# Token pairs for k and q of batch 0 and k of batch 1, one maximum and one exponential per part in batch 0, and another order of the head of a fused attention and MLP kernel

## The chip, the cores and the metric

One core of a Trainium2 chip runs the whole kernel. The metric is the device time of one execution in microseconds. Times of several executions are given as a median with the lowest and the highest. One further execution was taken by the hardware profiler; its time and its trace are used for the working, and they are a little longer than the median run. On this kernel a change of less than 0.2% cannot be told from none.

## The reference, cut to what matters

```python
# q, k, v: (8 batches, 8 heads, 576 tokens, 64);  p: (8, 8, 32, 64), float32
def sm_attn(qq, kk, vv):
    s = (1 / 8) * qq @ kk.T
    a = exp(s - max(s, axis=-1))
    a = a / (sum(a, axis=-1) + 1e-9)
    return a @ vv
p_packed = sm_attn(p, k, v)              # 32 packed rows per head
out = sm_attn(q, p_packed, p_packed)     # back to 576 tokens
x = out as (4608 tokens, 512)
h = x @ w_in                             # w_in (512, 1024), float64 in memory
solu = h * softmax(h)
ln = (solu - mean) / sqrt(var + 1e-6) * g_ln
return ln @ w_out                        # w_out (1024, 512), float64 in memory
```

## The kernel before, in words

**Steps and their order.** Every piece of work is a named step. `add` registers it with what it needs (`after`) and with the buffers that it takes and gives back; `perform` then emits the steps in the order of the long string `ORDER`, and `issue` ties each engine's instructions to that order. So an engine never overtakes itself: when a step waits, all that stands behind it on the same engine waits too. The loads, the transposing DMAs and the stores are all issued by SyncE (SP) in that order, into one queue. A name is step, then batch or `w` after a slash, or a token tile after a dash: `kt0/1` is for batch 1, `wa3/w` belongs to the weights, `m1-5` is for token tile 5.

**Weights (`/w`).** `w_in` and `w_out` come as 64-bit floats, in four pieces of 1 MB each: `lw0` to `lw3` for `w_in`, `lW0` to `lW3` for `w_out` (L215). For each piece, `wa` and `wl` take the high and the low word apart on ScalarE (ACT; L230, L234), `wm` joins the magnitude on VectorE (DVE; L239), `wp` sums columns on TensorE (PE; L249), and `ws` puts the sign in on DVE (L256). Two maxima follow: `wb` for `w_in` (L259) and `pw` for `w_out` (L316 to L322). For each of the eight slices of `w_out`, `ch`, `cm` and `cl` then make the fp16 high and low parts `wch` and `wcl` (L330, L340 to L343, L334).

**Attention of a batch (`/0` to `/7`).** The loads are `lk`, `lq` and `lv`. In batch 0, k and q are loaded as rows of token pairs for tokens 0 to 511 (L127, 512 bytes in a run) and two loads for the last 64 tokens (L135), turned by PE in the steps `ka` and `qa` (L151, L153) and copied by ACT in `kc` and `qc` (L159, L161). In all other batches k and q come in four parts each with runs of 128 bytes (L412), and DVE turns them in 32 by 32 blocks, four steps `kt` and four `qt` each (L428). `s10` and `s11` are the scores of the packed rows for even and odd heads (L441 for batch 0, L451 else), `mx` their row maxima (L456 for each half of 288 columns, L458 to join them), `ex` the exponentials (L469 for each half, with sums), `es` and `rs` the sums and their reciprocals. `tp`, `tc` and `av` turn the exponentials and multiply by v (L488, L495, L505). `pp` scales (L514), `pt` and `pc` turn the packed rows (L524, L528), `pe`, `pk`, `to` and `un` find a power-of-two unit (L519 to L359). `sx` are the second scores (L547, L554), `sb`, `sm`, `su`, `se`, `ss`, `sn` the second softmax (L559 to L579), `at`, `ah`, `al` give the weights as fp16 high and low parts `a2h` and `a2l` (L618 to L633). `z0` and `z1` multiply the packed rows by `w_in` (L590), `zh` and `zl` store the product as fp16 high and low parts (L606 on ACT, L614 on DVE).

**Token tile (36 of 128 tokens).** `m1` is h: 12 products of 128 by 512 into one of two h buffers (L721). `nm` is the row maximum (L725, L727), `bd` a bound (L733 to L736), `ex` the exponential on ACT (L741), `u` the product on DVE (L746), `mu` the mean on GpSimd (POOL; L750), `yh` and `yl` the fp16 high and low parts (L754, L757), `tr` a transposing DMA (L761), `sq` and `cr` the row factor (L765 to L773). `m2a` and `m2b` are the second product, 24 of 128 by 512, all into one PSUM buffer (`NPO = 1`, L780); `ev` scales and copies it out (L784), `st` stores it. The first four tiles (0 to 3) belong to batch 0; tile 4 is half of batch 0 and half of batch 1.

The shape of the head is thus: weights and batch 0's attention must come before the first `m1`; the parts of `w_out` must be ready before the first `m2a`.

Of the kernel before, what the change touches and what calls it, by code (L numbers as in the profile page):

```python
# [34 lines left out]
tp0/0 tc0/0 tp1/0 tc1/0 tp2/0 qa1/0 qa2/0 qc1/0 lW2/w wp4/w qa3/0 ws4/w lv/0 tc2/0 av/0 wa6/w wl6/w qc2/0 es1/0
rs/0 lW3/w qc3/0 wp5/w ws5/w lP/w wm6/w lk0/1 pp/0 pe/0 lk1/1 pt/0 pc/0 wp6/w ws6/w sx0/0 sb0/0 sm0/0 sx1/0
wa7/w sb1/0 pk/0 wl7/w wm7/w su0/0 z0/0 to/0 se0/0 un/0 z1/0 wp7/w zh0/0 pw/w ko/w lq0/1 sm1/0 su1/0 ch5/w
lk2/1 lq1/1 lq2/1 ch4/w cm4/w cm5/w se1/0 ss0/0 sn0/0 lk3/1 at0/0 pa/w ss1/0 ch2/w pd/w px/w cm2/w kt0/1 zl0/0
ch3/w ch0/w zh1/0 ah0/0 kt1/1 ch1/w kt2/1 sn1/0 cl2/w cm0/w at1/0 cl4/w cm3/w cl0/w ah1/0 cl3/w kt3/1 s10/1
zl1/0 al0/0 al1/0 cl5/w cm1/w m1-0 mx0/1 ex0/1 ws7/w es0/1 ch6/w s11/1 m1-3 lq3/1 cl1/w cm6/w qt0/1 nm-0 lv0/1  # L40
mx1/1 lk0/2 lv1/1 lv2/1 lk1/2 bd-0 qt1/1 qt2/1 qt3/1 ex-0 u-0 ex1/1 tp0/1 es1/1 rs/1 tp1/1 tc0/1 tc1/1 mu-0
tp2/1 tc2/1 av/1 nm-3 pp/1 ch7/w cm7/w pt/1 yh-0 yl-0 tr-0 bd-3 pc/1 m1-2 ex-3 sq-0 lk2/2 lk3/2 u-3 cl6/w mu-3
pe/1 cl7/w nm-2 gd/w lv0/2 sx0/1 sb0/1 sm0/1 m1-1 yh-3 yl-3 ex-2 pk/1 to/1 tr-3 su0/1 se0/1 bd-2 un/1 z0/1
zh0/1 sq-3 lq0/2 ss0/1 u-2 zl0/1 kt0/2 m2a-0 m2b-0 mu-2 yh-2 lq1/2 yl-2 sx1/1 cr-0 ev-0 sb1/1 sm1/1 sn0/1 st-0
kt1/2 su1/1 m2a-3 sq-2 cr-3 kt2/2 tr-2 z1/1 kt3/2 se1/1 ss1/1 zh1/1 m2b-3 zl1/1 at0/1 ev-3 sn1/1 ah0/1 al0/1
at1/1 ah1/1 s10/2 mx0/2 ex0/2 lq2/2 lq3/2 nm-1 ex-1 bd-1 m2a-2 al1/1 s11/2 mx1/2 ex1/2 m1-5 u-1 tp0/2 tp1/2
lv1/2 tc0/2 cr-2 qt0/2 lk0/3 tc1/2 tp2/2 nm-5 lk1/3 qt1/2 tc2/2 ex-5 m2b-2 bd-5 es0/2 mu-1 yh-1 st-3 es1/2
lv2/2 u-5 mu-5 rs/2 qt2/2 yh-5 av/2 pp/2 pe/2 yl-5 sq-5 qt3/2 m1-6 tr-5 pt/2 pc/2 pk/2 sx0/2 yl-1 nm-6 m1-4
sq-1 ev-2 sb0/2 bd-6 sm0/2 su0/2 to/2 sx1/2 sb1/2 sm1/2 un/2 su1/2 ex-6 u-6 mu-6 lv0/3 m2a-5 z0/2 zh0/2 nm-4
bd-4 m2b-5 tr-1 m1-7 lv1/3 cr-5 zl0/2 z1/2 se0/2 ev-5 ss0/2 sn0/2 yh-6 yl-6 sq-6 cr-1 lk2/3 lk3/3 kt0/3 kt1/3  # L50
st-2 m2a-1 se1/2 m2b-1 zh1/2 ex-4 lk0/4 kt2/3 tr-6 kt3/3 ss1/2 lq0/3 sn1/2 lq1/3 zl1/2 s10/3 at0/2 cr-6 ev-1
at1/2 ah0/2 al0/2 ah1/2 mx0/3 lv2/3 nm-7 st-1 ex0/3 es0/3 u-4 mu-4 ex-7 m2a-6 s11/3 mx1/3 m2b-6 ex1/3 bd-7
tp0/3 tp1/3 tp2/3 yh-4 ev-6 u-7 es1/3 lk1/4 st-5 yl-4 al1/2 tc0/3 tc1/3 tc2/3 lq2/3 lq3/3 m1-9 qt0/3 qt1/3 nm-9
# [816 lines left out]
```

## Time and profile before

| | |
|---|---|
| median of 3 runs | 417.19 us (416.96 to 417.67) |
| profiled execution, its own time | 420.75 us |
| span of its instructions | 418.9 us |
| busy share of the span | PE 92%, DVE 79%, ACT 60%, POOL 32% |
| mean granted PE clock | 0.983 |
| first `m1` / first `m2a` on PE | 60.81 us / 80.94 us |

PE's busy share counts each matmul to its modelled end, and matmuls overlap; how close PE is to its pace is read from the distance of successive matmuls of one form, not from the busy share.

### The profile page before, as it was taken

What the parts mean: (1) busy time and instruction counts of PE and PEld (TensorE: products, weight loads), DVE (VectorE), ACT (ScalarE), POOL (GpSimd) and SP (SyncE); (2) the same over time, 40 slices, a digit from 0 to 9 for tenths busy, and PEclk for the clock granted to TensorE, in tenths of its full rate; (3) what the DMA queues carried; (4) which work ended last, traced back from release to release, by engine and by line L of the source; (5) the groups of instructions that cost most, each with busy time, mean ns of one, the idle gap of its engine ahead of it and who ended that gap; (6) DMA issues with size and microseconds to landing.
All of it is one profiled execution on the core that took longest, in us unless ns stands there. A gap on an engine that the chain in (4) does not pass through costs nothing.

```text
span 418.9 us, 8114 instructions
## 1 busy us (share of the span) xinstructions
PE 385.6 (92%) x3064; PEld 177.2 (42%) x3064; DVE 330.2 (79%) x657; ACT 252.6 (60%) x437; POOL 133.9 (32%) x264
## 2 busy tenths in 40 slices
PE   5678579989999899999999999899999999999995
...
DVE  1678898899999978887898878898799768757610
...
GB/s 292 382 318 251 150 214 72 168 215 158 111 204 205 180 210 77 145 208 79 225 183 139 188 119 216 141 102 144 98 178 103 80 166 69 151 52 100 75 153 75
DMA packets 243383, 66.99 MB, mean 160 GB/s; under 512 B 216464, under 2 KB 236944, under 8 KB 242832
## 3 DMA queue, kind: packets, MB, share of 16 engines
...
q8 instruction: 24, 0.39, 0.4%
...
HBM read 37.23 MB, written 9.44 MB: 111 GB/s over the span
## 4 chain that ended last, share of the span: by engine, by line
PE 65%; DMA 8%; ACT 8%; DVE 7%; SPq 5%; issue 3%; POOL 2%; ACTq 0%; DVEq 0%; POOLq 0%
PE po L780 37%; PE h L721 18%; DMA yT<-yhl 4%; SPq L135 2%; SPq L412 2%; PE pa L590 2%; DMA zh<-in_moe_w_in_dram 2%; ACT o_sb L784 2%; PE pa L554 2%; PE pa L488 1%; DMA raw<-in_moe_w_out_dram 1%; DVE u L746 1%; ACT e L741 1%; PE pa L505 1%; DMA raw<-in_k_dram 1%
## 5 line engine op out<-in xcount | busy, mean ns | idle before, releaser
L780 PE MATMUL po<-wch,yT 128*128 128x512 f16 x576 | 179.4, 380 | 8.0 <-ACT o_sb L784 4.0
L780 PEld LDWEIGHTS <-yT 128*128 128x128 f16 x864 | 82.5, 98 | 119.4 <-issue 17.4
L780 PE MATMUL po<-wcl,yT 128*128 128x512 f16 x288 | 109.3, 379 | 0.0
L754 ACT ACTIVATE yhl<-u,negmu 128x1024 f16<-128x1024 f32 x36 | 41.3, 1146 | 30.5 <-POOL negmu L750 30.5
L725 DVE TENSOR_REDUCE nm<-h 128x1 f32<-128x1024 f32 x36 | 43.7, 1213 | 19.5 <-PE h L721 19.5
L741 ACT ACTIVATE e<-h,bias,unit 128x1024 f32<-128x1024 f32 x36 | 43.3, 1202 | 23.9 <-DVE bound L733 12.5
L721 PE MATMUL h<-zh,a2h 128*128 128x512 f16 (+1 forms) x160 | 55.4, 384 | 0.0
L721 PE MATMUL h<-zl,a2h 128*128 128x512 f16 (+1 forms) x160 | 55.2, 383 | 0.0
L757 DVE SCALAR_TENSOR_TENSOR yhl<-u,negmu,yhl 128x1024 f16<-128x1024 f32 x36 | 49.4, 1372 | 7.4 <-ACT yhl L754 6.5
L721 PE MATMUL h<-zh,a2l 128*128 128x512 f16 (+1 forms) x160 | 55.0, 381 | 0.0
L784 ACT ACTIVATE o_sb<-po,c_row 128x512 f32<-128x512 f32 x36 | 24.6, 682 | 48.4 <-PE po L780 27.3
L746 DVE SCALAR_TENSOR_TENSOR u<-e,s_row,h 128x1024 f32<-128x1024 f32 x36 | 45.5, 1266 | 5.8 <-ACT e L741 5.2
L750 POOL TENSOR_SCALAR negmu<-su 128x1 f32<-128x1 f32 x36 | 9.7, 271 | 104.7 <-DVE u L746 72.9
L721 PEld LDWEIGHTS <-a2h 128*128 128x128 f16 (+1 forms) x320 | 27.7, 101 | 36.1 <-issue 7.5
L765 ACT ACTIVATE e<-u,negmu 128x1024 f32<-128x1024 f32 x36 | 41.0, 1139 | 0.0
L772 POOL TENSOR_SCALAR c_row<-sq,k_out,s_eps 128x1 f32<-128x1 f32 x36 | 15.2, 423 | 43.1 <-ACT e L765 40.3
L566 POOL TENSOR_TENSOR s<-s,mx 128x576 f32<-128x576 f32 x14 | 18.0, 1291 | 24.8 <-DVE mx L563 24.8
L579 POOL TENSOR_TENSOR a<-a,sm 128x576 f32<-128x576 f32 x14 | 17.1, 1220 | 22.6 <-DVE sm L576 17.9
L469 ACT ACTIVATE e<-pa,nmx 128x288 f32<-128x288 f32 x28 | 13.7, 496 | 16.3 <-DVE nmx L458 12.8
L633 POOL TENSOR_TENSOR a2l<-s,a2h 128x576 f16<-128x576 f32 x14 | 18.3, 1318 | 11.8 <-ACT a2h L629 11.7
L773 POOL TENSOR_TENSOR c_row<-c_row,neg_half 128x1 f32<-128x1 f32 x36 | 21.0, 583 | 3.0
L721 PEld LDWEIGHTS <-a2l 128*128 128x128 f16 (+1 forms) x160 | 14.4, 101 | 17.1 <-DVE nmx L458 0.3
...
## 6 DMA issues: line engine op xcount, KB each, us to landing
...
```

Source lines behind the costliest of these rows:

```text
L566: (nc.gpsimd if b else nc.vector).tensor_tensor(out=st['w', r], in0=st['w', r], in1=st['mx', r].unsqueeze(2).broadcast_to([P, NB, J]), op= ...
L633: (nc.gpsimd if b or A2L_BY[r] == 'p' else nc.vector).tensor_tensor(out=lo, in0=a2T, in1=hi, op=ALU.subtract)
L721: nc.tensor.matmul(h[rows, 512 * n:512 * n + 512], lhsT=lhsT, rhs=z[:, r, 512 * n:512 * n + 512], start=t == 0, stop=t == end)
L725: nc.vector.tensor_reduce(out=nm, in_=st['h'], axis=AX.X, op=ALU.max, negate=True)
L741: nc.scalar.activation(st['e'], st['h'], AF.Exp, bias=st['bias'], scale=st['unit'][:, 1:2], accum_out=st['se'])
L746: nc.vector.scalar_tensor_tensor(out=st['u'], in0=st['e'], scalar=st['s_row'], in1=st['h'], op0=ALU.mult, op1=ALU.mult, accum_out=st['su'])
L754: nc.scalar.activation(st['y'][:, 0], st['u'], AF.Identity, bias=st['negmu'])
L757: nc.vector.scalar_tensor_tensor(out=st['y'][:, 1], in0=st['u'], scalar=st['negmu'], in1=st['y'][:, 0], op0=ALU.add, op1=ALU.subtract)
L765: nc.scalar.activation(st['e'], st['u'], AF.Square, bias=st['negmu'], accum_out=st['sq'])
L773: nc.gpsimd.tensor_tensor(out=c_row, in0=c_row, in1=neg_half, op=ALU.pow)
L780: nc.tensor.matmul(st['po'], lhsT=st['yT'][:, a, c], rhs=w[:, c], start=c == 0 and t == 0, stop=c == NFC - 1 and t == 2)
L784: nc.scalar.activation(st['o'], st['po'], AF.Copy, scale=st['c'])
```

## The change

- Batch 0's k and q and batch 1's k are loaded as token pairs (`ROWS`). The load is cut into three steps (`lk0`, `lk1` of 512 KB each, and `lk2` of four DMAs of 32 partitions). PE turns 128 by 128 blocks that hold two tokens of a head, so that the even tokens of the first 288 pairs stand in the upper half of the partitions and the odd ones in the lower half: 4 transposes and 2 small ones for a step `ka` or `qa`, where 16 products and one transpose stood. Batch 1's k goes by `ka` and `kc` (PE and ACT) and no longer by `kt` (DVE). Batch 0 uses the same `s1` and `s2` as the others, with p loaded for all 8 heads in each of its four DMAs.
- Batch 0's softmax takes one maximum over both halves and one exponential with its sum per part, and has no `es`.
- `ZL_PE = 1`: batch 0's low part of z is made by PE (`zm`: minus the high part, plus the scaled product once more) and copied by ACT. `PP_ACT = 2`: `pp` and `pc` of batches 0 and 1 go from DVE to ACT.
- `zh` and `zl` of batch 0 are copied 1024 columns at a time.
- `FILL` issues twelve fillers of three 128x512 bf16 matmuls each: `f0`, `f1`, `f11`, `f7`, `f4`, `f9`, `f8` in the head, `f3` and `f6` in the middle, `f2`, `f5`, `f10` at the end.
- `ORDER` is another one throughout. In the queue of loads, k of batch 0 now comes first, then `lw0`, `lw1`, p, `lw2`, one part of batch 1's k, q and v of batch 0, and `lw3`; before, it was `lw0`, `lw1`, k, `lw3`, `lw2`, p, `lW1`, q, `lW0`, v. The work on `w_out`, `wa4` and after, is moved behind most of batch 0's attention.
- Options that stay off (`S0_POOL`, `WS_POOL` and the like) change nothing.

```diff
-ROWS = 1
+ROWS = ('kq', 'k')
-ZL_PE = 0
-PP_ACT = 0
+ZL_PE = 1
+PP_ACT = 2
-FILL = [0, 0, 0, 0, 0, 0, 0, 0]
+FILL = [3, 3, 3, 3, 3, 3, 3, 3, 3, 3, 3, 3, 0, 0, 0, 0]
 ORDER = '''
-lw0/w wa0/w wl0/w wm0/w wp0/w lw1/w wa1/w wl1/w lk/0 wm1/w wp1/w lw3/w ws1/w lw2/w wa3/w wl3/w ws0/w ka0/0
...
+lk0/0 lk1/0 lk2/0 ka0/0 ka1/0 f7/w lw0/w kc0/0 ka2/0 wa0/w lw1/w kc1/0 kc2/0 ka3/0 wa1/w lp/w p0/w lw2/w kc3/0
+wl0/w wm0/w wl1/w s10/0 mx0/0 lk0/1 wm1/w ex0/0 s11/0 lq0/0 f0/w lq1/0 mx1/0 lq2/0 ex1/0 wp0/w lv0/0 rs/0 lv1/0
+lv2/0 lw3/w f1/w lP/w wp1/w ws1/w f11/w wa2/w tp0/0 qa0/0 qa1/0 ws0/w wl2/w tc0/0 wm2/w qc0/0 lk1/1 tp1/0 tc1/0
+tp2/0 tc2/0 qa2/0 av/0 lW0/w qc1/0 qc2/0 qa3/0 wa3/w wp2/w ws2/w wl3/w lk2/1 pp/0 pa/w pt/0 wm3/w wp3/w qc3/0
+ws3/w pe/0 pd/w wb/w pc/0 pk/0 to/0 un/0 wa4/w sx0/0 sx1/0 sb0/0 sb1/0 wl4/w us/0 sm0/0 su0/0 se0/0 ss0/0 ka0/1
+f4/w lW1/w ka1/1 kc0/1 kc1/1 px/w sm1/0 su1/0 f9/w wa5/w sn0/0 at0/0 ka2/1 ka3/1 lg/w kc2/1 se1/0 wl5/w lW2/w
+kc3/1 ah0/0 z0/0 z1/0 ss1/0 s10/1 zh0/0 zm0/0 sn1/0 at1/0 wm5/w ah1/0 lW3/w zh1/0 gm/w zm1/0 lv0/1 mx0/1 wm4/w
+ex0/1 wp4/w ws4/w s11/1 zl0/0 wp5/w es0/1 al0/0 mx1/1 zl1/0 al1/0 m1-2 wa6/w wl6/w ws5/w ex1/1 wa7/w tp0/1
...
+cr-2 nm-0 lk0/2 ch5/w sx0/1 sb0/1 sm0/1 lk1/2 su0/1 cl4/w cm5/w lk2/2 lk3/2 cl5/w kt0/2 kt1/2 lk0/3 lk1/3 sx1/1
+tr-2 se0/1 lk2/3 m2a-2 m2b-2 sb1/1 tr-3 sm1/1 su1/1 lk3/3 lv0/2 ss0/1 bd-1 sq-3 z1/1 se1/1 lq0/2 ss1/1 ev-2
...
+sq-33 u-31 tr-33 cr-33 m2b-32 m1-35 ev-32 st-32 mu-31 m2a-33 yh-31 yl-31 sq-31 cr-31 m2b-33 st-34 tr-31 nm-35
+ex-35 bd-35 u-35 mu-35 ev-33 m2a-31 m2b-31 yh-35 yl-35 st-33 f2/w ev-31 tr-35 sq-35 m2a-35 m2b-35 f5/w st-31
+f10/w cr-35 ev-35 st-35
 '''
...
+        for i in range(G):
+            nc.sync.dma_start(flat[32 * i:32 * i + 32, 2048:].rearrange('p (h x) -> p h x', h=2), src[2 * i:2 * i + 2, S - LEFT:, :].rearrange('h (p w) d -> p h (w d)', w=2))
...
+        for x in range(2):
+            pt = st[dst, g][x]
+            for c in range(2):
+                at = (c * H + 2 * g + x) * P
+                nc.tensor.transpose(out=pt[:, c * P:(c + 1) * P], in_=flat[:, at:at + P], identity=ident)
+            nc.tensor.transpose(out=pt[:, 2 * P:2 * P + 32], in_=flat[rows, 2048 + x * P:2048 + (x + 1) * P], identity=ident[rows, rows])
...
         def s1_max(r):
+            if not b:
+                nmx = st['nmx', r] = small.tile([P, 1], F32, name='nmx')
+                nc.vector.tensor_reduce(out=nmx, in_=st['s1', r][2][:, :, :HALF], axis=AX.XY, op=ALU.max, negate=True)
+                return
...
+            if not b:
...
+                nc.scalar.activation(st['e1'][:, r].rearrange('p (m n) -> p n m', n=2), st['s1', r][2][:, :, :HALF], AF.Exp, bias=st['nmx', r], accum_out=st['ssum'][:, r:r + 1])
+                return
...
         def z_low(n):
+            if b < ZL_PE:
+                nc.scalar.copy(st['z'][1][:, :, 512 * n:512 * n + 512], st['zp', n][2])
+                return
```

More of the change, by code (lines that the diff above doesn't have):

```diff
@@ L35 @@
[L35 to L53, printed above, removed]
-av/3 lq0/4 mu-7 bd-9 lk2/4 tr-4 m1-10 sq-4 yh-7 yl-7 cr-4 m2a-4 sq-7 rs/3 pp/3 tr-7 pe/3 pt/3 ex-9 lv0/4 u-9
@@ new lines @@
+m2a-20 tc0/6 m2b-20 tc1/6 st-17 bd-25 tc2/6 av/6 mu-22 qt2/6 yh-22 f6/w lk1/7 yl-22 tr-22 sq-22 ex-25 yl-26
+u-25 lv0/7 rs/6 pp/6 mu-25 yh-25 ev-20 st-15 m1-23 cr-22 pe/6 pt/6 pc/6 yl-25 qt3/6 nm-23 m1-24 lk2/7 lk3/7
+pk/6 sx0/6 sb0/6 sm0/6 su0/6 kt0/7 sq-26 bd-23 cr-26 ex-23 m2a-22 sx1/6 to/6 un/6 sb1/6 sm1/6 su1/6 m2b-22
+se0/6 ss0/6 ev-22 sq-25 se1/6 u-23 kt1/7 kt2/7 cr-25 z0/6 ss1/6 tr-26 sn0/6 m2a-26 zh0/6 mu-23 zl0/6 sn1/6
+yh-23 tr-25 st-20 kt3/7 m2b-26 yl-23 ev-26 z1/6 at0/6 ah0/6 st-22 tr-23 at1/6 ah1/6 zh1/6 nm-24 al1/6 sq-23
```

280 lines of the change are left out of this document (149 added, 131 removed).

## The prediction

> **What bounds the kernel now.** I read the page first, then busy time by stretch, the timeline of the head, the chain that ended last, and the groups by form.
>
> ```profile
> span 418.9 us, 8114 instructions
> PE 385.6 (92%) x3064; PEld 177.2 (42%) x3064; DVE 330.2 (79%) x657; ACT 252.6 (60%) x437; POOL 133.9 (32%) x264
> ...
> PE   5678579989999899999999999899999999999995
> ...
> DVE  1678898899999978887898878898799768757610
> ```
>
> The first tenth is where PE is far from full; from the eighth slice on it looks full. The stretches are cut at the places where the product of the tiles begins:
>
> ```profile
> core 0: us, PE busy (x) PEld busy (x) DVE busy (x) ACT busy (x) POOL busy (x), PEclk, DMA share, GB/s
> 0.00:28.10 28.10, 17.86 (x157) 13.01 (x158) 14.01 (x20) 18.36 (x31) 0.91 (x8) 0.88 0.96 326
> 28.10:60.80 32.70, 22.86 (x245) 10.27 (x244) 28.24 (x53) 23.78 (x44) 1.02 (x4) 0.93 1.02 224
> 60.80:80.90 20.10, 19.82 (x197) 9.34 (x195) 18.20 (x40) 14.09 (x29) 1.74 (x4) 0.94 0.57 111
> 80.90:414.90 334.00, 324.91 (x2476) 144.61 (x2468) 269.73 (x547) 195.71 (x333) 130.23 (x249) 1.00 0.69 144
> 4.00:6.00 2.00, 1.91 (x13) 1.74 (x12) 0.00 (x0) 0.13 (x1) 0.00 (x0) 1.00 0.99 377
> 38.00:40.00 2.00, 1.30 (x33) 0.69 (x25) 1.69 (x4) 1.07 (x2) 0.00 (x0) 1.00 0.90 144
> 100.00:110.00 10.00, 9.72 (x123) 5.51 (x121) 9.51 (x22) 8.48 (x16) 0.97 (x5) 1.00 0.18 48
> ```
>
> ```profile
> 5.87 1.12 ACT L230 ACTIVATE e<-zh 128x1024 f32<-128x1024 f32 x1 [3.46 <-DMA zh<-in_moe_w_in_dram]
> ...
> 17.40 1.18 ACT L230 ACTIVATE e<-zh 128x1024 f32<-128x1024 f32 x1
> ...
> 60.81 0.64 PE L721 MATMUL h<-zh,a2h 128*128 128x512 f16 x1
> ...
> 80.94 0.39 PE L780 MATMUL po<-wch,yT 128*128 128x512 f16 x1
> ```
>
> The head to the first `m1` (60.8) is bound by DVE and by what feeds it: DVE is busy 14.0 of 28.1 us while loads arrive, then 28.2 of 32.7. The DMA queue is full all this time (share 0.96 and 1.02).
>
> How much work PE has left is read from the chain, in rows where matmuls follow without a wait:
>
> ```profile
> 334.80 1.17 PE pa L488 x10
> ...
> 341.15 1.66 PE pa L505 x80
> ...
> 348.32 0.65 PE pa L554 x16
> ...
> 355.23 1.02 PE pa L590 x16
> ...
> 373.02 5.18 PE po L780 x24
> ...
> 388.79 2.59 PE h L721 x12
> ...
> 402.76 0.70 ACT o_sb L784
> ```
>
> A tile costs 2.59 + 5.18 = 7.77 us. A batch costs 1.17 + 1.66 + 4 x 0.65 (`s1`, taken like `sx`) + 2 x 1.02 = 7.5, some 7.9 with the small turns. At 80.94 `m1` of four tiles is done, and of batch 1 all but one `sx` and one `z`. Left: 36 x 7.77 - 4 x 2.59 + 6 x 7.9 + 1.67 = 318.4 us. The span has 338.0 us left, so 19.6 us are lost: 4.0 behind the last product (414.9 to 418.9), about 3 in the tail where each product waits for the copy-out of the one before (the 0.70 row; one PSUM buffer), some 12.6 in between. Of those:
>
> ```profile
> PEld L780 <- DMA yT<-yhl: 8.7, 6, 2.4
> ...
> PE po L780 <- DMA yT<-yhl: 4.0, 4, 1.5
> PE po L780 <- ACT o_sb L784: 4.0, 7, 1.1
> ```
>
> So the end is set by two things: when PE has its first `m2a` with the same work done, and how much of the 12.6 us comes back. The time of the first `m1` alone decides nothing.
>
> **The change part by part.** The durations:
>
> ```profile
> L428 DVE STREAM_TRANSPOSE kT<-raw 128x576 f32<-128x576 f32 x28 | 20.2, 750 | 0.9 <-DMA raw<-in_k_dram 0.9
> L614 DVE SCALAR_TENSOR_TENSOR zl<-h,unit,zh 128x512 f16<-128x512 f32 x4 | 2.7, 724 | 0.0
> L456 DVE TENSOR_REDUCE mx<-h 128x1 f32<-128x288 f32 x4 | 1.6, 451 | 0.2 <-PE h L441 0.2
> L563 DVE TENSOR_REDUCE mx<-s 128x18 f32<-128x576 f32 x16 | 12.0, 748 | 0.3
> L239 DVE SCALAR_TENSOR_TENSOR e<-e,u 128x1024 int32<-128x1024 int32 x8 | 9.6, 1212 | 11.4 <-ACT u L234 11.4
> L514 DVE TENSOR_SCALAR pp<-pa,rs 128x128 f32<-128x128 f32 x16 | 4.9, 346 | 0.6 <-PE pa L505 0.3
> L469 ACT ACTIVATE e<-h,nmx 128x288 f32<-128x288 f32 x4 | 2.0, 497 | 0.1
> L725 DVE TENSOR_REDUCE nm<-h 128x1 f32<-128x1024 f32 x36 | 43.7, 1213 | 19.5 <-PE h L721 19.5
> L741 ACT ACTIVATE e<-h,bias,unit 128x1024 f32<-128x1024 f32 x36 | 43.3, 1202 | 23.9 <-DVE bound L733 12.5 <-DVE bias L727 9.1 <-PE pa L505 2.0
> L746 DVE SCALAR_TENSOR_TENSOR u<-e,s_row,h 128x1024 f32<-128x1024 f32 x36 | 45.5, 1266 | 5.8 <-ACT e L741 5.2
> L754 ACT ACTIVATE yhl<-u,negmu 128x1024 f16<-128x1024 f32 x36 | 41.3, 1146 | 30.5 <-POOL negmu L750 30.5
> L757 DVE SCALAR_TENSOR_TENSOR yhl<-u,negmu,yhl 128x1024 f16<-128x1024 f32 x36 | 49.4, 1372 | 7.4 <-ACT yhl L754 6.5
> ```
>
> *Loads.* The first piece of `w_in` is used at 5.87: some 3 us of start and landing, and 1.05 MB at 377 GB/s. Batch 0's k (1.18 MB) now comes first, at about 6.2 us; `lw0` follows at 9.0, `lw1` at 11.8, `lw2` behind p at 15. One part of batch 1's k, q and v stand ahead of `lw3`: 8.4 MB up to its end is 25 to 26 us by the same rate, where the last piece of `w_in` was used at 17.40. So `w_in` goes back in the queue, not forward. `lW0` lands at about 33 and `lW3` at about 43; SP issues `px` (four DMAs) among them, behind `pd`. The four small DMAs for the last tokens replace two with half the runs; I count the issues on SP at nothing, because the queue of data is what SP waits for; if that cover goes, four issues more per load. Batch 1's k in runs of 512 bytes can move at the 326 GB/s of the first stretch, not at the 144 of 38 to 40 us, when only 128-byte runs flowed: 3.6 us of a full queue instead of 8.2. POOL gets nothing new before batch 1.
>
> *DVE up to the first `m1`.* Before: 14.0 + 28.2 = 42.2. Gone or moved behind: two `wm` and two `ws` (4 x 1.21 = 4.85), four `kt/1` (3.0), four `zl/0` (2.9), `pp` and `pc` (2 x 0.35 + 0.4, the copy taken like one `pp` and a little = 1.1), four half maxima against two whole ones (4 x 0.45 - 2 x 0.75 = 0.3); moved ahead: three half maxima of batch 1 (1.35). Left: 31.4. The reduction over two PSUM halves at once has no row; it lies between 0.75 and 0.90 each, and I take 0.75, since L563 has its width.
>
> *ACT takes it over*: two low parts of z of 1024 columns (1.15 each by L754), eight copies of 288 for batch 1's k (0.45 each, a little under L469), `pp` and `pc` of two batches (six at about 0.35), less the shorter exponentials and the separate copies of the last tokens. That is 8.0 less some 2: about +6 us before the first `m2a`, on an engine that was busy 56.2 of 80.9 us there. I count it as hidden beside DVE; if ACT is the later one, up to 3 us (half of it) come on top.
>
> *Where this ends.* Walking the order: k's copies and `wa0`, `wa1`, `wl0` stand in a row on ACT, so DVE's first `wm` starts near 14.4 (before: 8.0). DVE then waits for `lw3` by way of `wa3` and `wl3`, until about 28.1, and has done some 9.8 of its 31.4 by then. From there 21.6 remain to the first `m1`. At DVE's share between 0.88 (46.4 of 52.8 us from 28.1 to 80.9) and 0.95 (100 to 110) that is 51 to 53 us, against 60.8.
>
> That gain is not kept. Between the first `m1` and `m2a-2`, DVE now has five pieces of `w_out` work (6.1), the small chains of batch 1 and of `w_out`'s scale (about 2.8), four `nm` with bias (5.6), two `bd` (1.1), two `u` (2.5), two `yl` (2.7), four `qt` (3.0), `zl0/1` (1.5) and `sb0/1` (0.9), together 26.2, because `sx1/1` stands ahead of `m2a-2` on PE and needs `sb0/1`. ACT has about as much. PE has only some 25 us of work here, four `m1`, most of batch 1 and the eight `cm`. So `m2a-2` starts at 28.1 + 47.8 / (0.88 to 0.95) = 78.4 to 82.4, plus 0.65 for `sx1/1`. A walk with each wait gives 79.3; I take 80.4, and then 0.65 of PE work more is done than before at 80.94: -0.5 and -0.65.
>
> *Fillers.* Three matmuls at 5.18 / 24 are 0.65 us. Those in the head and in the tail lie in PE's idle time; `f3` and `f6` stand where PE is full: +1.3.
>
> *The stalls.* In the old order tiles 5, 32 and 24 have 12.4, 13.0 and 14.5 us of PE work between the end of `m1` and the start of `m2a` (adding the rows above along the order); a tile's own way there is 1.2 + 1.2 + 1.3 + 1.15 + 1.4 (`nm`, `ex`, `u`, `yh`, `yl`) and the transposing DMA:
>
> ```profile
> yT<-yhl SPq DMA_TRANSPOSE x36, 3.9
> ```
>
> That is 10.2, some 11.5 with `mu` and the hand-overs, before any queueing. In the new order the least is 16.7 (tile 7) and 17.6 (22), apart from tile 35 at the very end (11.1, with two copy-outs beside it). DVE has some 5 us less to do after the first `m2a`. Of the 12.6 us I take 2.5 as saved (between none and 6: the 4.0 on yT, and part of what the early queueing of DVE costs).
>
> *Clock.* The first six products at 60.81 came at 0.43 us apart instead of 0.216, 1.3 us lost after an idle PE. The new order has `zm` and `s1` right ahead of the first `m1`, which is no longer the limit; I take 0. The Trainium skill ("TensorE: Matmul & The Clock Gate", Part 1) says that an idle window of about 3.4 us halves the clock and that a busy one restores it; a filler of three matmuls is a fifth of such a window, so by that rule the fillers need not keep the clock up, and PE's pieces between DVE steps would take up to twice as long. No run here shows it.
>
> *Sum.* 420.75 - 0.5 - 0.65 + 1.3 - 2.5 = 418.4 for the profiled execution. The median run was 3.56 below it (417.19): 414.8.
>
> **The rivals.**
> 1. *The head counts for more* (first `m2a` at 78.4 + 0.65, stalls 6 us less): -1.9 - 0.65 + 1.3 - 6 = 409.9. For it: more slack in every tile. Against it: DVE stays 0.81 busy after 80.9, and PE lost time in places that no DVE wait explains.
> 2. *PE starves between `m1` and `m2a`* and the kernel gets slower. Mechanism: `lw3` behind q and v holds ACT, then DVE; all of `w_out` follows late, and only four tiles' `m1` can fill PE. At DVE's share of 0.88 and `lw3` 2 us later, `m2a-2` starts at 85: +4.1 - 0.65 + 1.3 - 1.2 = 420.7. It decides from a first `m2a` near 83.6 on. For it: 0.88 is what DVE reached here, and ACT is now as full. Against it: fewer small hand-overs in batch 0.
> 3. *Nothing to be measured*: the savings of DVE are returned by `w_in`'s later landing and by the fillers, the stalls come back elsewhere: 416.4 to 418.0.
>
> **How the numbers follow.** The forecast (410.5 to 416.4) gets 0.42, rival 1 gets 0.10, rival 3 0.15, rival 2 0.33. The range takes in both rivals' times with their bounds: 408 to 422. Faster 0.52, same 0.15 (within 0.2%, 0.8 us), slower 0.33.
>
> **What would show it.** Right: first `wm` (L239's successor) near 14 us, `wa3` near 26, first `m1` at 50 to 53, DVE and ACT both over 0.85 busy from 28 to 80, the first `m2a` at 79 to 82, no `kt/1` and fewer waits on yT after it. Wrong: a first `m2a` past 84, or before 77; a `w_in` piece that lands late for another reason; more than 15 us lost by PE after the first `m2a`; PE's matmuls at half pace in the head.

## The result, and the profile after

The changed kernel takes 423.08 us (median of 4 runs, 421.35 to 424.93), the kernel before 417.43 (416.96 to 418.63): a ratio of 1.0127, 95% interval 1.0100 to 1.0153. It is slower by 5.65 us, where 414.8 was forecast. One execution each of `d_turn_mm_win` and `f_old_relief` below fell in a slower state of the chip and is left out of their ratios, though not of their medians. The profiled execution took 424.93 us with a span of 423.1; that of before had 418.9.

The page of the changed kernel:

```profile
span 423.1 us, 8100 instructions
PE 403.2 (95%) x3069; PEld 182.4 (43%) x3072; DVE 321.0 (76%) x637; ACT 256.7 (61%) x436; POOL 126.2 (30%) x265
...
DVE  0538798998968999889988876867789888657340
...
PEclk9695599999999999999999999999999999999999
```

DVE has 9 us less work in all than before (321.0 against 330.2), and yet the kernel is longer. In the clock row the fourth and fifth slice stand at a half.

The busy time by stretch, cut at the fourth `wm`, the first `m1` and the first `m2a` of the changed kernel (columns as in the table of the prediction: length, PE, PEld, DVE, ACT, POOL, clock, DMA share, GB/s):

```profile
0.00:31.46 31.46, 24.77 (x210) 15.70 (x212) 9.94 (x15) 17.21 (x26) 0.92 (x9) 0.87 0.97 289
31.46:55.77 24.31, 22.68 (x171) 8.43 (x173) 19.94 (x35) 18.37 (x29) 0.46 (x2) 0.60 1.05 304
55.77:85.39 29.62, 27.51 (x223) 12.29 (x221) 27.26 (x51) 25.23 (x49) 4.90 (x13) 1.00 0.62 104
85.39:423.10 337.71, 328.24 (x2475) 145.93 (x2467) 263.83 (x539) 195.88 (x335) 119.96 (x242) 1.00 0.68 141
```

and the kernel before, cut at the same 31.46, at its own first `m1` and its first `m2a`:

```profile
0.00:31.46 31.46, 20.40 (x192) 14.96 (x192) 15.57 (x23) 21.72 (x37) 0.91 (x8) 0.89 0.97 331
31.46:60.81 29.35, 20.33 (x213) 8.31 (x209) 26.69 (x51) 20.42 (x38) 1.02 (x4) 0.92 1.02 207
60.81:80.94 20.13, 19.85 (x197) 9.34 (x196) 18.23 (x40) 14.09 (x29) 1.78 (x4) 0.94 0.57 111
```

The first `m1` comes 5.0 us earlier (55.77 against 60.81), the first `m2a` 4.45 later (85.39 against 80.94), and behind it both need the same (337.7 and 338.0). So the loss lies ahead of the first `m2a`, where DVE had 60.5 us of work and 20.5 of waits before the change, and has 57.1 of work and 28.2 of waits after it: 3.3 us of work saved, 7.8 us of waits added. The first 31.46 us show most of it: DVE does 9.94 us there instead of 15.57.

The waits, in the timelines of DVE and of ACT (start, duration, engine, line, and in brackets the idle time ahead and what ended it):

```profile
13.39 0.29 DVE L289 TENSOR_SCALAR o_sb<-o_sb 128x256 f32<-128x256 f32 x1 [11.82 <-DMA o_sb<-in_p_dram]
...
31.46 1.23 DVE L232 SCALAR_TENSOR_TENSOR e<-e,u 128x1024 int32<-128x1024 int32 x1 [5.35 <-ACT u L227]
...
46.23 0.75 DVE L597 TENSOR_REDUCE sm<-a 128x18 f32<-128x576 f32 x1 [1.98 <-ACT a L593]
```

```profile
29.30 1.12 ACT L223 ACTIVATE e<-zl 128x1024 f32<-128x1024 f32 x1 [2.81 <-DMA zl<-in_moe_w_in_dram]
...
31.31 0.63 ACT L542 ACTIVATE pp<-pa,rs 128x128 f32<-128x128 f32 x2
...
42.05 0.64 ACT L159 COPY kT<-h 128x576 f32<-128x576 f32 x1 [1.46 <-PE h L152]
...
44.97 0.64 ACT L159 COPY kT<-h 128x576 f32<-128x576 f32 x1 [1.24 <-PE h L152]
45.51 0.69 ACT L593 ACTIVATE a<-s 128x576 f32<-128x576 f32 x1
```

The first DVE wait is the load of p behind k and two pieces of `w_in`; the 5.35 is the last piece of `w_in`, for which ACT stands still and `pp` behind it; the 1.98 comes from ACT's copies of batch 1's k, which wait for PE's turns. On PE, a filler stands ahead of each of the two turns that ACT waits for:

```profile
39.03 1.46 PE L279 MATMUL pa<-ones_b 128*128 128x512 bf16 x3
40.28 0.63 PE L151 MATMUL h<-ident,raw 128*128 128x128 f32 x2
...
41.95 1.46 PE L279 MATMUL pa<-ones_b 128*128 128x512 bf16 x3
43.20 0.63 PE L151 MATMUL h<-ident,raw 128*128 128x128 f32 x2
```

These are `f4` and `f9`, 1.46 us each at a granted clock of 0.50 (40 to 46 us), where the prediction had 0.65 us in PE's idle time.

### The profile page after: what moved, and what is told of

It reads as the page before. It is cut to its first block, busy times and chain, and to the rows that moved or that the text cites. A ratio compares the mean times of both kernels' runs of the same rounds, so it can differ in the third digit from the quotient of the medians.

```text
span 423.1 us, 8100 instructions
## 1 busy us (share of the span) xinstructions
PE 403.2 (95%) x3069; PEld 182.4 (43%) x3072; DVE 321.0 (76%) x637; ACT 256.7 (61%) x436; POOL 126.2 (30%) x265
## 4 chain that ended last, share of the span: by engine, by line
PE 71%; DVE 13%; DMA 5%; ACT 5%; SPq 3%; issue 3%; POOL 0%; DVEq 0%; ACTq 0%; POOLq 0%
PE po L807 36%; PE h L748 18%; DMA zl<-in_moe_w_in_dram 3%; PE pa L613 3%; PE pa L470 2%; DVE nm L752 2%; DVE qT L454 2%; DVE u L773 2%; PE pa L361 2%; PE pa L577 2%; DMA out_dram<-o_sb 1%; PE pa L279 1%; SPq L137 1%; DVE yhl L784 1%; PE pa L535 1%
## 5 line engine op out<-in xcount | busy, mean ns | idle before, releaser
L784 DVE SCALAR_TENSOR_TENSOR yhl<-u,negmu,yhl 128x1024 f16<-128x1024 f32 x36 | 45.8, 1280 | 18.5 <-ACT yhl L781 18.4
L777 POOL TENSOR_SCALAR negmu<-su 128x1 f32<-128x1 f32 x36 | 7.8, 217 | 115.5 <-DVE u L773 109.5
L602 POOL TENSOR_TENSOR a<-a,sm 128x576 f32<-128x576 f32 x14 | 16.2, 1157 | 17.5 <-DVE sm L599 14.3
L632 ACT ACTIVATE zh<-pa,unit 128x512 f16<-128x512 f32 x28 | 17.6, 680 | 5.2 <-PE pa L613 4.3
```

The lines of the kernel that those rows point to most:

```text
L632: nc.scalar.activation(st['z'][0][:, r, 512 * n:512 * n + 512], st['zp', n][r], AF.Copy, scale=units[b][:, 0:1])
L784: nc.vector.scalar_tensor_tensor(out=st['y'][:, 1], in0=st['u'], scalar=st['negmu'], in1=st['y'][:, 0], op0=ALU.add, op1=ALU.subtract)
```

## The experiments

All runs are compared with runs of the kernel before on the same chip (medians of 417.7 to 418.5 us). DVE's work and waits are counted up to the first `m2a`, in the profiled execution.

### Fillers, the last piece of w_in, and the clock

**`a_no_fill`**: `FILL = [0, 0, ...]`, all else as in the change.

> The changed kernel with all twelve fillers empty. My prediction's step: two of them stand where PE is full, so 1.3 us less, the rest is free. Theory 2 (the clock): if the fillers keep PE's clock up in the head, it now falls earlier than 31 us and the head gets longer by 1 to 3 us; if they do nothing for it, the head is the same and the time falls by about 1.3 us.

Measured: 419.24 us, ratio 1.0041 (1.0017 to 1.0066). First `m1` 52.68, first `m2a` 82.27, behind it 335.33; DVE's waits 25.3. So the fillers cost 3.8 us by the medians (3.6 by the two ratios), three times the 1.3 of the prediction; 2.9 of DVE's 28.2 us of waits are theirs. Without them the kernel is still slower than before by 0.4%. Where that rest stands is seen when both are cut at 30.72, where the fourth `wm` of `a_no_fill` starts: first the kernel before, then `a_no_fill`, each up to there and from there to its first `m2a`.

```profile
0.00:30.72 30.72, 19.66 (x180) 14.30 (x182) 14.83 (x21) 20.98 (x35) 0.91 (x8) 0.89 0.97 330
30.72:80.94 50.22, 40.92 (x420) 18.31 (x418) 45.66 (x92) 35.25 (x69) 2.80 (x8) 0.93 0.84 171
...
0.00:30.72 30.72, 24.26 (x200) 15.95 (x200) 9.94 (x15) 17.32 (x26) 0.92 (x9) 0.83 0.96 293
30.72:82.27 51.55, 46.31 (x384) 19.32 (x385) 47.03 (x85) 43.55 (x77) 5.37 (x15) 0.87 0.87 204
```

Behind 30.72 DVE waits the same in both, 4.6 us before (50.22 - 45.66) and 4.5 in `a_no_fill` (51.55 - 47.03). All of the added waits lie ahead of it, 20.8 against 15.9, and the two longest of them go back to loads:

```profile
13.14 0.29 DVE L289 TENSOR_SCALAR o_sb<-o_sb 128x256 f32<-128x256 f32 x1 [11.58 <-DMA o_sb<-in_p_dram]
...
30.72 1.23 DVE L232 SCALAR_TENSOR_TENSOR e<-e,u 128x1024 int32<-128x1024 int32 x1 [4.84 <-ACT u L227]
```

The first ends with p's load, behind which the first `wm` follows only at 15.01, because ACT has k's copies to do as well. The second is ACT's work on the last piece of `w_in`, for which ACT itself waits until 28.55. So 4.9 us of DVE's work are not done while the loads arrive, and 3.5 us of work are saved.

**`a_no_f4_f9`**: only those two are gone.

> The changed kernel with only the fillers f4 and f9 gone (two groups of three matmuls, in front of the turns of batch 1's k on PE); the other ten stay. Theory F (these two hold ACT's copies of k and then DVE at half the clock): first m2a at 82.5 to 83.5 instead of 85.4, time 420 to 421. Theory G (each filler costs its share of the 3.8 us that all twelve cost): first m2a 84.5 to 85.5, time 422 to 423. By the prediction's step (fillers in the head lie in PE's idle time): no change, 423.

Measured: 421.19 us, 1.0085 (1.0064 to 1.0107); first `m2a` 81.06. ACT's timeline between 38 and 44 us:

```profile
38.44 1.16 ACT L159 COPY kT<-h 128x576 f32<-128x576 f32 x2
...
40.94 0.64 ACT L159 COPY kT<-h 128x576 f32<-128x576 f32 x1
...
43.09 0.65 ACT L159 COPY kT<-h 128x576 f32<-128x576 f32 x1
```

The waits of 1.46 and 1.24 are gone, and the last copy starts at 43.09 instead of 47.12. Two of twelve fillers make half of their whole cost, 1.9 of 3.8 us. That is nearest to theory F, though the first `m2a` comes earlier and the time is a little longer than its ranges. That these two lie in idle time, as the prediction had it, is wrong. The other ten cost nothing ahead of the first `m2a` (81.06, against 82.27 without any filler); behind it the part takes 337.8, against 335.3 without any.

**`a_lw3_early`**: one token of `ORDER`.

```diff
- ... lp/w p0/w lw2/w kc3/0 ... lv2/0 lw3/w f1/w ...
+ ... lp/w p0/w lw2/w lw3/w kc3/0 ... lv2/0 f1/w ...
```

> The changed kernel with one edit: the fourth piece of w_in is loaded right behind the third, ahead of batch 1's first part of k and of q and v of batch 0; the order on PE, DVE and ACT stays. Theory 1 (the load order): DVE's wait of 5.35 us for that piece goes, the first second product comes 3 to 5 us earlier than 85.4, and the time falls by 2.5 to 4 us, to about 419 to 420.5. Theory 2 (PE's half clock from 31 to 52 us by itself): the wait goes, but the clock stays at half and the first second product comes less than 1.5 us earlier. Theory 3 (too much work on ACT): the same, because ACT is what is late from 50 on.

Measured: 422.66 us, 1.0116 (1.0079 to 1.0152), no different from the change; first `m2a` 83.84, 1.55 earlier, which is between the ranges of the theories.

```profile
30.22 1.13 ACT L223 ACTIVATE e<-zl 128x1024 f32<-128x1024 f32 x1
...
32.42 1.23 DVE L232 SCALAR_TENSOR_TENSOR e<-e,u 128x1024 int32<-128x1024 int32 x1 [6.39 <-ACT u L227]
```

ACT no longer waits for the load (no bracket), but takes the piece only at 30.22: the turns of q and of the exponentials, whose loads are later now, stand ahead of it. DVE's wait is 6.39 instead of 5.35. What gets shorter is the stretch behind it: from the fourth `wm` to the first `m2a` it is 51.42 us instead of 53.93. In this execution the granted clock was 0.98 from 36 to 46 us, and `f4` and `f9` are short:

```profile
39.76 0.82 PE L279 MATMUL pa<-ones_b 128*128 128x512 bf16 x3
...
41.45 0.82 PE L279 MATMUL pa<-ones_b 128*128 128x512 bf16 x3
```

Without `f4` and `f9` the same stretch takes 51.13 us (29.93 to 81.06). So it looks as if these two cost time ahead of the first `m2a` only because the clock is at half where they stand; this rests on one profiled execution of each kernel.

**`c_w3_front`**: without fillers, `lw3` behind `lw2`, batch 1's first part of k behind v, and `wa2 wl2 wm2 wa3 wl3 wm3` moved right behind `ex1/0`, so ahead of those copies.

> The changed kernel without fillers; k stays first as in the change, but lw3 stands right behind lw2, batch 1's first k part goes behind v, and ACT's wa2, wl2, wa3, wl3 stand ahead of the copies of batch 0's exponentials and of q (wm2, wm3, wp2, ws2, wp3, ws3 move with them). Moving lw3 alone gained nothing for DVE, since ACT's order stood. Theory A: now the fourth wm runs at 24 to 27 instead of 31 to 34, first m1 at 50 to 52, first m2a 79 to 81, time 416 to 418 (without fillers and with the old places: 419.2). Theory B: first m2a stays at 81.5 to 83, time 418.5 to 420, because softmax and q are later by what w_in is earlier.

Measured: 424.53 us, 1.0146 (1.0123 to 1.0168); first `m2a` 86.28, waits 29.1. Slower by 5.3 than without this edit (4.4 by the two ratios). The fourth `wm` came at 28.4 (expected 24 to 27), and `pp` at 35.6 instead of 30.6. Neither theory had that.

**`c_win_first`**: without fillers, the steps of `w_in` and batch 0's k in the order of the kernel before (`lw0 wa0 wl0 wm0 wp0 lw1 wa1 wl1 lk0/0 lk1/0 lk2/0 wm1 wp1 lw3 ...`).

> The changed kernel without fillers, and its head in the order of the kernel before: lw0, lw1 and their wa, wl, wm, wp ahead of batch 0's k; lw3 and lw2 ahead of p and q; every other token in the order of the changed kernel. To be compared with the changed kernel without fillers (first m2a 82.3 us, 419.2 us). Theory A (w_in's late landing starves DVE in the first 30 us, and this idle time never comes back): the wait of 5 to 6 us for the fourth wm goes, first m1 at 48 to 51, first m2a at 77 to 79.5, time 414 to 416.5, below the kernel before. Theory B (what bounds is the chain of hand-overs among ACT, DVE and PE between 30 us and the first m2a, whatever the order of loads): first m2a 81 to 83, time 418 to 420.

Measured: 425.58 us, 1.0179 (1.0160 to 1.0199); first `m2a` 88.28.

```profile
22.70 1.22 DVE L252 SCALAR_TENSOR_TENSOR w_in_sb<-zl,e 128x1024 int32<-128x1024 int32 x1
...
37.90 0.29 DVE L549 TENSOR_REDUCE peak<-pp 128x1 f32<-128x128 f32 x1 [10.07 <-ACT pp L542]
```

The last `ws` of `w_in` starts at 22.70 instead of 31.98 in `a_no_fill`, and DVE then waits 10.07 us for `pp`; the first piece of `w_out` lands at 35.5, so there is nothing else to be done. Theory A's forecast fails: when the piece comes early, the wait changes its place and grows. The edit also puts batch 0's k behind two pieces of `w_in`, so it does not test the late piece alone.

**`e_pp_first`**: without fillers, `qc3/0 pp/0 pt/0 pe/0 pc/0 pk/0` moved ahead of `wa3`.

> The changed kernel without fillers (419.2; DVE begins batch 0's second softmax at 35.6, first m1 52.7, first m2a 82.3), and on ACT and PE the last copy of q, pp, its turn, copy and peak stand ahead of wa3, which waits for the last piece of w_in (it lands at 28.5, and ACT stands still behind it while pp is ready at about 28). Theory D with ACT's order as the cause of the late softmax: second softmax from 31 to 33, first m1 at 49 to 51, first m2a 29.5 to 30 later, 78.5 to 81, time 415.5 to 418. Rival: what comes later on DVE (the fourth wm, ws, w_in's bound) only changes places with the softmax, since DVE needs both before the first m1: first m2a 81.5 to 82.5, time 418.5 to 419.5.

Measured: 424.58 us, 1.0141 (1.0113 to 1.0170); the second softmax starts at 40.2 instead of 35.6, first `m2a` 86.55. On DVE it stands behind the last `wm` and `ws` of `w_in` and its bound, and the fourth `wm` now comes at 35.50. Both sides were missed.

**`a_fill_long`**: `f4` and `f9` with 10 matmuls, and a filler of 14 behind `wl3`.

> The changed kernel with longer fillers in the head: 14 matmuls in PE's idle time at 28.5 us (a new filler), 10 instead of 3 in the two at 39 and 42 us. Theory 2 (the clock): it stays at full from 31 to 52 us, turns of k and the z products there take half, the first second product comes 2 to 4 us earlier. Theory 1 (the load order): DVE still waits until 31.5 for the last piece of w_in; the first second product moves by less than 1.5 us either way. Known cost if the clock stays low: 14 added matmuls at 0.43 us, 6 us of PE's time where it has some to spare.

Measured: 425.52 us, 1.0189 (1.0153 to 1.0224). The clock from 20 to 55 us rose from 0.71 to 0.90, and the time got worse; the first `m2a` came at 86.07. But the edit adds 28 matmuls, 14 of them ahead of turns that ACT waits for, where a filler takes 2.33 us instead of 1.46. It does not price the clock by itself.

**`d_turn_mm`, `d_turn_mm_nofill`, `d_turn_mm_win`**: in the change, without fillers, and in `c_win_first`, one line.

```diff
- nc.tensor.transpose(out=pt[:, c * P:(c + 1) * P], in_=flat[:, at:at + P], identity=ident)
+ nc.tensor.matmul(pt[:, c * P:(c + 1) * P], lhsT=flat[:, at:at + P], rhs=ident, start=True, stop=True)
```

> The changed kernel with one line different: the turns of 128x128 blocks of k and q on PE are ordinary matmuls against the identity (as in the kernel before) instead of PE's transposes; order, fillers and all else as in the change. Theory H: in the change PE is busy in the head but its granted clock stays at a half (0.5 from 30 to 51 us) because most of what it does there are transposes, which don't count as work for the clock; so every PE piece between two DVE steps takes twice as long. Then: clock from 20 to 55 us at 0.85 or more on average (0.6 to 0.7 before this edit), first m1 at 51 to 53 instead of 55.8, first m2a at 80 to 82.5 instead of 85.4, time 418 to 420.5. Theory A (only the late loads and ACT's order count, the clock is a side show): clock no matter, first m2a 84.5 to 86.5, time 422.5 to 424.5, since these matmuls are no shorter than the transposes.

> The same edit, and no fillers (compare with the changed kernel without fillers: 419.2 us, first m2a 82.3). Theory H: clock 0.8 or more from 20 to 55 us without any filler, first m2a 78.5 to 80.5, time 415.5 to 417.5, as fast as the kernel before or faster. Theory A: first m2a 82 to 83.5, time 419 to 420.5. A third possibility: without fillers and with few matmuls the clock falls again in the waits, and the result lies between, 417.5 to 419.

> The same edit in the kernel with w_in's loads first and no fillers (425.6 us, first m2a 88.3, clock 0.5 from 28 to 52 us with PE nearly always busy there). Theory H: the order of loads looked bad only because PE turned k and q at half the clock in one stretch: clock 0.85 or more from 20 to 50, first m2a 79 to 82.5, time 416 to 419.5. Not H: 424 to 427, first m2a 87 to 89.

**`d_b_transpose`**: the reverse in the kernel before.

> The reverse: the kernel before, with the turns of batch 0's k and q as PE's transposes of 128x128 blocks (four for each turn, instead of eight matmuls of half the width). The blocks are taken as they lie in memory, so the heads come out in another layout and the values are not those of the reference; the work of every engine is the same. Theory H: clock from 20 to 40 us falls from 1.0 to 0.5 to 0.7, first m1 at 62.5 to 65 instead of 60.8, first m2a 82.5 to 85 instead of 80.9, time 419 to 421.5. Theory A: no change, 416.5 to 418.5.

Measured: 425.86 us (422.17 to 427.15; 1.0177, 1.0138 to 1.0216), 423.56 (1.0129, 1.0089 to 1.0170), 430.06 (1.0279, 1.0252 to 1.0307), and 417.67 for the reverse (0.9994, 0.9978 to 1.0010). The stretch from 20 to 55 us of the change, of `d_turn_mm`, of the kernel before and of `d_b_transpose`:

```profile
20.00:55.00 35.00, 30.72 (x290) 13.89 (x289) 24.12 (x39) 24.85 (x38) 0.46 (x2) 0.71 1.03 289
...
20.00:55.00 35.00, 31.10 (x328) 18.28 (x327) 26.43 (x45) 26.82 (x42) 0.46 (x2) 0.95 1.02 285
...
20.00:55.00 35.00, 25.14 (x300) 13.53 (x301) 29.37 (x55) 28.57 (x57) 1.02 (x4) 0.95 1.00 240
...
20.00:55.00 35.00, 25.36 (x238) 12.24 (x239) 29.44 (x55) 27.88 (x54) 1.02 (x4) 0.81 0.98 230
```

Half of theory H holds: with the turns as matmuls the clock is 0.95 where it was 0.71, and with them as transposes it is 0.81 where it was 0.95. (Without fillers it rose only from 0.71 to 0.75, with `w_in` first from 0.59 to 0.81.) The other half, that this sets the time, got no support: none of the three kernels with matmul turns became faster (the two without fillers became slower), the one with transposes did not become slower, and the first `m2a` came at 84.65, 85.09, 91.87 and 79.27. But the runs do not refute it either, because the edit makes a turn longer. Two blocks of a turn in the change, at a clock of 0.99 and then of 0.50, and in `d_turn_mm` at 1.00:

```profile
21.98 0.44 PE L151 MATMUL h<-ident,raw 128*128 128x128 f32 x2
22.53 0.44 PE L151 MATMUL h<-ident,raw 128*128 128x128 f32 x2
...
44.01 0.69 PE L151 MATMUL h<-ident,raw 128*128 128x128 f32 x2
44.87 0.69 PE L151 MATMUL h<-ident,raw 128*128 128x128 f32 x2
...
22.07 0.71 PE L151 MATMUL h<-ident,raw 128*128 128x128 f32 x4
22.88 0.71 PE L151 MATMUL h<-ident,raw 128*128 128x128 f32 x4
```

From start to start this is 0.55 us as transposes at full clock, 0.86 at half, and 0.81 as matmuls at full clock: two matmul records stand there for each block, where a transpose has one. So the edit gains almost nothing where the clock was half, and loses 0.26 us for each pair of blocks where it was full. In the kernel before it is the same: a turn takes 1.09 us as matmuls at full clock, and in `d_b_transpose` 1.12 as transposes at half (26.8 to 28 us, clock 0.50). What the half clock costs the turns was not measured.

### Order or code

The sums up to the first `m2a`, one row for each: the kernel before, the change, `a_no_fill`, `e_old_order` and `f_old_relief`. DVE's work is its busy time, its waits are the rest of the length.

```profile
0.00:80.94 80.94, 60.58 (x596) 32.62 (x597) 60.48 (x112) 56.23 (x103) 3.71 (x16) 0.92 0.89 231
...
0.00:85.39 85.39, 74.96 (x603) 36.42 (x606) 57.14 (x99) 60.81 (x102) 6.28 (x24) 0.84 0.87 229
...
0.00:82.27 82.27, 70.58 (x584) 35.28 (x585) 56.97 (x99) 60.86 (x102) 6.29 (x24) 0.85 0.90 237
...
0.00:81.50 81.50, 63.60 (x504) 31.80 (x509) 59.97 (x106) 55.21 (x89) 3.66 (x17) 0.79 0.88 228
...
0.00:86.11 86.11, 66.17 (x540) 32.15 (x544) 57.07 (x100) 58.75 (x98) 4.53 (x17) 0.84 0.87 224
```

**`c_k1_cols`**: without fillers, `ROWS = ('kq', '')`, so batch 1's k goes by DVE again.

> The changed kernel without fillers, and k of batch 1 as before the change (32-row pieces, four transposes on DVE of 0.75 us instead of turns on PE and eight copies on ACT). Theory A (DVE's lost time decides): DVE has 3.0 us more to do before the first m2a, which comes at 84 to 85.5; time 420.5 to 422. Theory C (ACT was given too much, and PE's turns at half the clock hold it): first m2a 79.5 to 81.5, time 416.5 to 418.5.

Measured: 421.24 us, 1.0080 (1.0063 to 1.0097); DVE's work 59.6, waits 25.7, first `m2a` 85.23. Against `a_no_fill` 2.6 us more work and 0.4 more waits: inside this order DVE's work does count, as theory A had it (420.5 to 422): the time is 2.0 us longer.

**`b_lw2_late`**: the kernel before, with `lw2` loaded behind q and v.

```diff
- lw2/w ... lp/w ... lq/0 ... lv/0
+ lq/0 lv/0 ... lw2/w ... lp/w
```

> The kernel before with one edit: its last piece of w_in is loaded behind q and v of batch 0 (p stays ahead), as in the changed kernel. Theory 1: the third and fourth signed pieces come some 6 us later, DVE waits, the first second product moves from 80.9 to about 84 to 86, and the time rises by 3 to 5 us. Theories 2 and 3: within 1 us of before, since neither the clock nor ACT's work is touched.

The edit put p behind q and v too, which the expectation says it did not. Measured: 425.77 us, 1.0187 (1.0152 to 1.0222); waits 27.5 instead of 20.5, first `m2a` 87.66. So in the kernel before, late loads of this kind cost 8 us; p's share in it isn't parted from `lw2`'s.

**`b_wout_late`**: the kernel before, with `lW0` to `lW3` behind v, and the first three pieces of `w_out` (`wa` to `ws`) behind `sx1/0`.

> The kernel before with w_out alone late: its four loads behind v of batch 0, and its first three pieces (wa, wl, wm, wp, ws) behind the first part of the second softmax, as the changed kernel has them. Theory D: second softmax from 32 to 36 instead of 38.7 (v lands earlier), first m1 at 54 to 60, from there to the first m2a 23 to 28 us instead of 20.1, first m2a at 82 to 86 instead of 80.9, time 419.5 to 423. Rival (the late w_out is made up for by the earlier q and v): first m2a 80 to 81.5, time 416.5 to 418.5.

Measured: 425.61 us, 1.0165 (1.0138 to 1.0192); first `m2a` 87.40, DVE's work 60.5, waits 26.9.

```profile
35.30 0.61 DVE L514 TENSOR_SCALAR pp<-pa,rs 128x128 f32<-128x128 f32 x2 [5.71 <-PE pa L505]
...
38.17 0.85 DVE L559 STREAM_TRANSPOSE s<-h 128x288 f32<-128x288 f32 x2 [1.40 <-PE h L547]
```

In the kernel before, the same transpose of the second softmax:

```profile
38.73 0.85 DVE L559 STREAM_TRANSPOSE s<-h 128x288 f32<-128x288 f32 x2 [0.27 <-PE h L547]
```

With `w_out` out of the way v lands 8 us earlier (about 26.1 instead of 34.1), and the second softmax starts only 0.56 us earlier, since the chain of turns and copies on PE and ACT was the later one. What DVE had done in that time it now waits. The price of deferral is as theory D had it (waits +6.4), its place is not: 7.4 us came ahead of the first `m1` (68.22), and from there to the first `m2a` it is 19.2 us, not 23 to 28.

**`e_old_order`**: the new code for batch 0 in the whole order of the kernel before; `ROWS = ('kq', '')`, `ZL_PE = 0`, `PP_ACT = 0`, no fillers.

> The new code for batch 0 (token pairs for k and q, one maximum and one exponential per part) in the whole order of the kernel before, without fillers; batch 1's k, the low part of z and pp as before the change. It parts what the code does from what the order does. Theory D (deferral): the loss is the order's: w_out's loads stand behind q, v and batch 1's k, so five pieces of w_out that DVE did while it waited for loads now lie between the first m1 and m2a, a stretch that took 29.5 to 32.8 us in every kernel with the new order and 20.1 in the kernel before. Then here: first m1 58 to 60.5, first m2a 78 to 81, time 415 to 418.5. Theory L: the code of the pairs is itself the slower one (transposes on PE at half the clock, strided exponentials): first m2a 82.5 to 86, time 420 to 424.

Measured: 418.80 us, ratio 1.0003 (0.9982 to 1.0023); DVE's work 60.0, waits 21.5, first `m2a` 81.50. Theory D's range for the first `m2a` was 78 to 81 and its time up to 418.5, so both are just outside it, and the first `m1` at 62.41 is later than its 58 to 60.5; theory L's time (420 to 424) is farther off. In this order the new code of the pairs, the single maximum and the single exponential of batch 0 cost nothing that can be measured, and bring nothing.

**`e_old_order_all`** and **`f_old_relief`**: the same order with all of the new code, and with `ZL_PE = 1` and `PP_ACT = 2` alone.

> The whole new code (pairs for batch 1's k too, the low part of z by PE and ACT, pp on ACT for two batches) in the order of the kernel before, without fillers. Theory D: DVE has some 6 to 7 us less to do before the first m2a than in the kernel before and waits no more than there; first m2a 76 to 79.5, time 413 to 417. Theory C (ACT was given too much, and the moved steps come out slower there): first m2a 81 to 84, time 418 to 422.

> The order of the kernel before with the new code of batch 0 (418.8 us, first m2a 81.5: DVE's work 60.0, waits 21.5), and in it the low part of z by PE and ACT and pp on ACT for two batches, as in the change; batch 1's k stays on DVE, and there are no fillers. If DVE's sum decides and the old order lets it work while loads arrive: work 56, waits 21.5 to 23, first m2a 77.5 to 79.5, time 414.5 to 417, faster than both kernels. Rival (DVE's relief turns into waits for ACT and PE, as it did in the change): waits 25 or more, first m2a 81 to 83, time 418 to 420.5.

Measured: 435.82 us (1.0388, 1.0355 to 1.0422) with DVE's work at 54.4 and its waits at 41.5; and 423.19 us (1.0106, 1.0079 to 1.0134) with work at 57.1 and waits at 29.0. Two rows of the second show how relief becomes a wait:

```profile
73.38 0.63 ACT L542 ACTIVATE pp<-pa,rs 128x128 f32<-128x128 f32 x2 [1.47 <-PE pa L535]
...
75.97 1.28 DVE L784 SCALAR_TENSOR_TENSOR yhl<-u,negmu,yhl 128x1024 f16<-128x1024 f32 x1 [2.33 <-ACT yhl L781]
```

`pp` of batch 1, now on ACT, waits there for PE, and `yh` of a token tile stands behind it; DVE, relieved of `pp`, waits 2.33 us for `yh`.

**`f_k1_late`**: the change with the four fillers `f7 f0 f1 f11` alone, and `lk0/1` behind `lw3`.

> The changed kernel with two repairs: the fillers but for the four ahead of the first softmax's end (f7, f0, f1, f11) are gone, and batch 1's first k part is loaded behind lw3 instead of ahead of q. Sum that the runs so far suggest: first m2a = DVE's work up to it + DVE's waits up to it (57.2 + 28.2 in the change; 56.9 + 24.2 with f4 and f9 gone; 60.5 + 20.4 in the kernel before). The earlier lw3 should take 1 to 1.5 us off the wait for the fourth wm (about 4 us): waits 22.5 to 23.5, first m2a 79.5 to 80.5, and 335.3 behind it, as without fillers: 415.5 to 417.5. Rival (DVE's wait only moves to what lands next, as in every edit of the loads so far): waits 24 to 26, first m2a 81 to 83, time 417.5 to 419.5.

Measured: 420.39 us, 1.0055 (1.0035 to 1.0075); waits 25.4, first `m2a` 82.52: the rival's range for the waits, and a time above both ranges. The fourth `wm` runs at 29.57 instead of 30.7, and the wait comes back at 39.84 (2.09 us for ACT). No version beat the kernel before; the best with the new code, `e_old_order`, equals it.

## Why the prediction was wrong, point by point

In the 20 profiles the part behind the first `m2a` takes 334.8 to 338.0 us, and the first `m2a` lies between 79.3 and 96.0. So the frame of the prediction, the first `m2a` plus what follows, was right, and its first term was wrong. For the profiled execution it had 418.4, and 424.93 was measured: of these 6.5 us, 5.0 stand ahead of the first `m2a` and 1.6 behind it (337.7, where 338.0 - 0.65 + 1.3 - 2.5 = 336.15 was forecast).

- *First `m2a` at 80.4* (measured 85.39). Two steps failed. The last piece of `w_in` was to be there at 25 to 26 and the fourth `wm` at 28.1; ACT takes the piece at 29.30, the fourth `wm` starts at 31.46 (30.7 without fillers). That is 3.4 of the 5.0 us. The rate of 377 GB/s came from a stretch with whole pieces of weights; with k, q and v among them the first 31.46 us run at 289, and 8.4 MB at that rate are 29.1 us. From there the prediction had 47.8 us of DVE's work at a share of 0.88 to 0.95; measured are 47.2 us at 0.875 (19.94 + 27.26 in 53.9), against some 0.92 behind the 80.4 that was taken: the other 1.6 us. Without fillers it is 0.91 (47.0 in the 51.5 from its fourth `wm` at 30.72 to 82.27), so the share was right for the kernel without them, and what failed here is the price of `f4` and `f9` at half the clock.
- *First `m1` at 51 to 53*: 55.77 with fillers, 52.68 without.
- *Fillers, +1.3*: 3.8. The cover that was named, PE's idle time in the head, isn't there at 39 to 43 us, where PE's turns feed ACT and ACT feeds DVE.
- *Stalls behind the first `m2a`, -2.5*: of this size by the profiles, but not shown. Without fillers the part is 335.3 instead of 338.0, that is -2.7, and PE's own waits on yT (4.0 us before) are gone from the list; the fillers give 2.4 of it back. But the profiled run of before was 3.3 us above its median, and `d_b_transpose` and `e_old_order`, which take the same time as before, have 336.4 and 336.1 there, so a part of the 2.7 belongs to that one execution.
- *Clock, 0*: it fell to 0.60 between 31.46 and 55.77, as the prediction's own list of signs of being wrong had it. The Trainium skill ("TensorE: Matmul & The Clock Gate", Part 4) says that transposes don't count as work for the clock in the way matmuls do, and the runs agree (0.71 against 0.95); that was not weighed. Zero was wrong where `f4` and `f9` stand (1.46 us each instead of 0.82 in `a_lw3_early`). What the clock costs beyond that is open: without fillers it is 0.87 behind the fourth `wm`, where DVE waits no longer than in the kernel before, and of the edits meant to raise it none made the kernel faster.
- *The size of the miss against the median*: the profiled executions differ by 4.2 us, the medians by 5.65. The profiled run of before was 3.3 us above its median, that of after 1.85; the prediction carried the first offset over, with 3.56; that is the other 1.7 of the 8.3 us between 414.8 and 423.08.
- *Rival 2* named the mechanism (PE starves, the first `m2a` past 83.6, `lw3` behind q and v holding ACT and then DVE) and was given 0.33. It put the first `m2a` at 85 and the time at 420.7; its time was too low by about what the fillers cost beyond 1.3. That its 85 fits so well is in part luck, since it had no price for the fillers in the head.

What is shown: the code of the token pairs costs nothing in the old order; the fillers make 3.8 of the 5.65 us, half of it by the two at 39 and 42 us; the loss of the head stands as waits of DVE, and without fillers all that is added to them lies ahead of the fourth `wm`, where the two longest go back to loads. Work taken from DVE came back as waits in the old order (`f_old_relief`), and batch 1's k taken from DVE in the new one is worth 2 us (`c_k1_cols`). What is only made likely by `b_wout_late` and `c_win_first`: that the rest, 0.4%, comes from putting `w_out` behind q and v (in the kernel before `lW1`, `lW0` and also `lW2` stand ahead of v), so that DVE has nothing to do while loads arrive and batch 0's chain runs over PE and ACT. The experiment that would settle it, the new order with `w_out` loaded and worked on early, was not run.
